# A two-phase recurrence and gated feed-forward kernel: the second phase's products in plain fp32 in place of three rounded products

## The chip, the cores and the metric

The kernel runs on one core of a Trainium2 chip. The metric is device time in microseconds (us) of one execution; lower is better. Engines are called as the profile calls them: PE is TensorE (matmul; PEld its weight loads), DVE VectorE, ACT ScalarE, POOL GpSimd, SP the engine that issues the DMAs (SPq in the profile).

## The reference

The first part is a recurrence over 768 steps for 4 batches x 8 heads with a 40 x 40 state; the second is a feed-forward block whose gate mixes along the sequence.

```python
for t in range(S):                                     # phase one
    y[:, :, t] = einsum('bhd,bhde->bhe', rt, state)
    Sa = einsum('bhde,bhe->bhd', state, at)
    state = state * wt[:, :, None, :] - Sa (x) bt + vt (x) kt
x = y as [batch 4, seq 768, 320]

h = maximum(x @ w_in, 0.0)                             # w_in 320 x 1024
u, v = h[..., :512], h[..., 512:]
v_n = (v - mean(v)) / sqrt(var(v) + 1e-06)
v_s = einsum('ts,bsd->btd', w_spatial, v_n) + b_spatial[None, :, None]   # phase two
return (u * v_s) @ w_out                               # w_out 512 x 320
```

All inputs and outputs are fp32; the two weight matrices w_in and w_out arrive as pairs of 32-bit words of float64 and are decoded on the chip.

## The kernel before

**Phase one** (`phase1`) computes the recurrence in 24 steps of 64 sequence positions, for two batches at a time, with many small fp32 matmuls (lines 536 to 638: 32 to 104 columns, 32 to 128 rows) and copies by ACT between them. Its order is a plan written out by hand: each operation has a due time, and the plan is sorted. Between the steps it also computes u and v (`m_u`, L753, and `m_v`, L708) for blocks of 128 positions, normalises v, and stores both to DRAM tensors `uts` and `vns`. For the second pair of batches this goes on after the last step, so that phase one has a tail. That tail and the second phase are ordered by the framework's scheduler, which places instructions by simulated time and interleaves the two.

**Phase two** (`phase2`) goes through 4 batches x 2 halves of the sequence (TH = 384 positions).

- Preparation: the six 128 x 768 tiles of the transposed w_spatial are loaded to a staging tile `raw` and split into a rounded high part `wsh` (ACT, `split_hi`, L50) and the remainder `wsl` (DVE, `split_lo`, L54). The four 128 x 320 blocks of w_out are decoded by `decode64` (seven DVE steps), and split into `woh` and `wol` in its last three operations (L96 to L98, one on ACT and two on POOL). Parts are of type fp32r, a rounded fp32 type that the matmul takes.
- `vload(b)` loads batch b's six 128 x 512 tiles of v to `raw`, splits each into `vh` (ACT) and `vl` (POOL), and loads u (`ut`). Tiles are kept for two batches; batch b+1 is loaded after the first half of batch b.
- `spatial(b, h)` makes four products pg (128 x 384), each a sum over six tiles of three matmuls: high x high (L173), high x low (L174), low x high (L175). DVE adds the bias (L177) and multiplies by u (L178) to give g; ACT and POOL split g into `gh` and `gl`.
- `proj(b, h)` makes three products po (128 x 320), each a sum over four blocks of three matmuls (L193). ACT copies them out (L194), and one DMA stores them. It is called one half late, so that the next half's spatial products stand ahead of it.

Counted over the whole phase this is 4 x 2 x 4 x 6 x 3 = 576 matmuls of 384 columns and 4 x 2 x 3 x 4 x 3 = 288 of 320 columns. Every DMA named is issued by SP, in one queue. The pools of phase two take memory that phase one's tiles used, and a tile waits for the tiles that were there.

Of the kernel before, what the change touches and what calls it, by code (L numbers as in the profile page):

```python
# [8 lines left out]
F32 = mybir.dt.float32  # L9
F32R = mybir.dt.float32r  # L10
# [4 lines left out]
ALU = mybir.AluOpType  # L15
# [3 lines left out]
P = 128  # L19
# [12 lines left out]
DH = 512  # L32

@with_exitstack
def tile_kernel(ctx, tc, early, late, vtok, win, wspT, bsp, wout, out):
    nc = tc.nc
    dram = ctx.enter_context(tc.tile_pool(name="dram", bufs=1, space=DRAM))
    B = out.shape[0]
    S = out.shape[1]
    xs = dram.tile([B, 2, NP, E, S], F32, name="xs")  # L40
    vns = dram.tile([B, S // P, P, DH], F32, name="vns")
    uts = dram.tile([B // NB, S // P, DH // P, P, NB, P], F32, name="uts")
    with ExitStack() as c1:
        phase1(c1, tc, early, late, vtok, win, xs, vns, uts, dram)
    with ExitStack() as c2:
        phase2(c2, tc, vns, uts, wspT, bsp, wout, out)


def split_hi(eng, hi, x):
    eng.activation(hi, x, AF.Copy)  # L50


def split_lo(eng, lo, x, hi):
    eng.tensor_tensor(out=lo, in0=x, in1=hi.bitcast(F32), op=ALU.subtract)  # L54


def decode64_steps(nc, pool, h, l, src, n, bufs=1):
    raw = pool.tile([P, n], I64, name="d_raw", bufs=2)
    nc.sync.dma_start(out=raw, in_=src)
    yield  # L60
    words = raw.bitcast(I32).rearrange("p (n two) -> p n two", two=2)
    lo, hi = words[:, :, 0], words[:, :, 1]
    t = [pool.tile([P, n], I32, name=f"d_t{i}", bufs=bufs) for i in range(3)]
    nc.vector.tensor_scalar(
        out=t[0], in0=hi, scalar1=3, scalar2=0x7FFFFFFF,
        op0=ALU.logical_shift_left, op1=ALU.bitwise_and,
    )
    yield
    nc.vector.tensor_scalar(
        out=t[1], in0=hi, scalar1=-0x80000000, scalar2=0x40000000,  # L70
        op0=ALU.bitwise_and, op1=ALU.bitwise_xor,
    )
    yield
    nc.vector.tensor_tensor(out=t[0], in0=t[0], in1=t[1], op=ALU.bitwise_xor)
    yield
    nc.vector.tensor_scalar(
        out=t[1], in0=hi, scalar1=0x7FFFFFFF, scalar2=None, op0=ALU.bitwise_and
    )
    yield
    f1 = t[2].bitcast(F32)  # L80
    nc.vector.scalar_tensor_tensor(
        out=f1, in0=t[1], scalar=float(897 << 20), in1=t[0].bitcast(F32),
        op0=ALU.is_ge, op1=ALU.mult,
    )
    yield
    nc.vector.tensor_scalar(
        out=t[0], in0=t[2], scalar1=-0x800000, scalar2=None, op0=ALU.bitwise_and
    )
    yield
    f2 = t[1].bitcast(F32)  # L90
    nc.vector.scalar_tensor_tensor(
        out=f2, in0=lo.bitcast(U32), scalar=2.0 ** -52, in1=t[0].bitcast(F32),
        op0=ALU.mult, op1=ALU.mult,
    )
    yield
    split_hi(nc.scalar, h, f1)  # L96
    nc.gpsimd.tensor_tensor(out=f1, in0=f1, in1=h.bitcast(F32), op=ALU.subtract)
    nc.gpsimd.tensor_tensor(out=l, in0=f1, in1=f2, op=ALU.add)  # L98


def decode64(*args, **kw):
    for _ in decode64_steps(*args, **kw):
        pass


def phase2(ctx, tc, vns, uts, wspT, bsp, wout, out):
    nc = tc.nc
    B, S, DO = out.shape
    NT = S // P
    TH = S // 2  # L110
    ND = DH // P

    def pool(name, bufs, **kw):
        return ctx.enter_context(tc.tile_pool(name=name, bufs=bufs, reuse_waits="tile", **kw))

    wstg = pool("p2r", 1)
    wsp = [pool(f"ws{i}", 1) for i in range(NT)]
    const = pool("p2c", 1)
    vp = [[pool(f"va{i}", 1, side="right") for i in range(NT)], None]
    up = [pool("ua", 1), None]  # L120
    stg = pool("p2s", 2)
    wp = pool("p2w", 2)
    vp[1] = [pool("vb", 1)] * NT
    up[1] = pool("ub", 1)
    ps_s = [pool(f"ps_s{i}", 2, space=PSUM) for i in range(2)]
    ps_o = pool("ps_o", 3, space=PSUM)

    wsh, wsl = [None] * NT, [None] * NT
    for i in range(NT):
        raw = wstg.tile([P, S], F32, name="raw", bufs=2)  # L130
        nc.sync.dma_start(out=raw, in_=wspT[i * P:(i + 1) * P])
        wsh[i] = wsp[i].tile([P, S], F32R, name=f"wsh{i}")
        wsl[i] = wsp[i].tile([P, S], F32R, name=f"wsl{i}")
        split_hi(nc.scalar, wsh[i], raw)
        split_lo(nc.vector, wsl[i], raw, wsh[i])
    woh = const.tile([P, ND, DO], F32R, name="woh")
    wol = const.tile([P, ND, DO], F32R, name="wol")
    for k in range(ND):
        decode64(nc, wstg, woh[:, k], wol[:, k], wout[k * P:(k + 1) * P], DO)
    bb = const.tile([P, S], F32, name="bb")  # L140
    nc.sync.dma_start(out=bb, in_=bsp.broadcast_to([P, S]))

    ut, vt = {}, {}

    def vload(b):
        vt[b] = []
        for i in range(NT):
            raw = wstg.tile([P, S], F32, name="raw", bufs=2)[:, 0:DH]
            nc.sync.dma_start(out=raw, in_=vns[b, i])
            vpool = vp[b % 2][i]  # L150
            h = vpool.tile([P, DH], F32R, name=f"vh{b % 2}{i}")
            l = vpool.tile([P, DH], F32R, name=f"vl{b % 2}{i}")
            split_hi(nc.scalar, h, raw)
            split_lo(nc.gpsimd, l, raw, h)
            vt[b].append((h, l))
        ut[b] = up[b % 2].tile([P, ND, S], F32, name=f"ut{b % 2}")
        for i in range(NT):
            nc.sync.dma_start(
                out=ut[b][:, :, i * P:(i + 1) * P],
                in_=uts[b // NB, i, :, :, b % NB].rearrange("d p t -> p d t"),  # L160
            )

    def spatial(b, h):
        ts = slice(h * TH, (h + 1) * TH)
        gh = wp.tile([P, ND, TH], F32R, name="gh")
        gl = wp.tile([P, ND, TH], F32R, name="gl")
        for d in range(ND):
            dc = slice(d * P, (d + 1) * P)
            pg = ps_s[d % 2].tile([P, TH], F32, name=f"pg{d % 2}")
            for i in range(NT):  # L170
                vh, vl = vt[b][i]
                w_h, w_l = wsh[i][:, ts], wsl[i][:, ts]
                nc.tensor.matmul(pg, lhsT=vh[:, dc], rhs=w_h, start=(i == 0), stop=False)  # L173
                nc.tensor.matmul(pg, lhsT=vh[:, dc], rhs=w_l, start=False, stop=False)  # L174
                nc.tensor.matmul(pg, lhsT=vl[:, dc], rhs=w_h, start=False, stop=(i == NT - 1))  # L175
            g = stg.tile([P, TH], F32, name="g")
            nc.vector.tensor_tensor(out=g, in0=pg, in1=bb[:, ts], op=ALU.add)  # L177
            nc.vector.tensor_tensor(out=g, in0=g, in1=ut[b][:, d, ts], op=ALU.mult)  # L178
            split_hi(nc.scalar, gh[:, d, :], g)
            split_lo(nc.gpsimd, gl[:, d, :], g, gh[:, d, :])  # L180
        return gh, gl

    def proj(b, h, gh, gl):
        ot = stg.tile([P, TH // P, DO], F32, name="ot")
        for j in range(TH // P):
            tc_ = slice(j * P, (j + 1) * P)
            po = ps_o.tile([P, DO], F32, name="po")
            mm = []
            for d in range(ND):
                mm += [(gh[:, d, tc_], woh[:, d, :]), (gh[:, d, tc_], wol[:, d, :]),  # L190
                       (gl[:, d, tc_], woh[:, d, :])]
            for i, (l, r) in enumerate(mm):
                nc.tensor.matmul(po, lhsT=l, rhs=r, start=(i == 0), stop=(i == len(mm) - 1))  # L193
            nc.scalar.activation(ot[:, j, :], po, AF.Copy)  # L194
        nc.sync.dma_start(
            out=out[b, h * TH:(h + 1) * TH].rearrange("(j p) n -> p j n", p=P), in_=ot
        )

    vload(0)
    pend = None  # L200
    for b in range(B):
        for h in range(2):
            gg = spatial(b, h)
            if b + 1 < B and h == 0:
                vload(b + 1)
            if pend is not None:
                proj(*pend)
            pend = (b, h, *gg)
    proj(*pend)


def phase1(ctx, tc, early, late, vtok, win, xs, vns, uts, dscr):
# [455 lines left out]
    def decode(half, k):  # L668
        cs = slice(half * DH, (half + 1) * DH)
        yield from decode64_steps(nc, st["dec"], wh[:, k, cs], wl[:, k, cs], win[:, k, cs], DH)  # L670
# [338 lines left out]
```

## Time and profile before

| what | value |
|---|---|
| median of 3 runs | 708.72 us (706.22 to 714.5) |
| profiled execution | span of 709.5 us from the first to the last instruction; the page lists no other time for it |
| instructions | 26133 |
| PE busy | 593.6 us (84%), 11136 matmuls |
| DVE busy | 437.5 us (62%) |
| ACT busy | 414.7 us (58%) |
| POOL busy | 290.3 us (41%) |
| mean granted TensorE clock | 0.900 |
| first and last matmul of phase two | start at 523.7 and 705.0 us |

A page of the profile lists busy time by engine, the span in 40 slices (a digit is the busy share in tenths), and groups of instructions by line of the kernel. In a group's row come line, engine, operation, output and inputs by tile names, shapes and count, then busy time in us and the mean duration of one in ns, then the idle time of the engine ahead of them and what ended it. The duration of a matmul reaches from its start to its modelled end and overlaps the next one's, so what one costs in a dense stream is the distance of starts. A row of the timeline has start, length, engine, line, operation and count; a row of the chain of work that ended last has start, its share of the chain's time, engine, tile, line and count.

### The profile page before, as it was taken

What the parts mean: (1) busy time and instruction counts of PE and PEld (TensorE: products, weight loads), DVE (VectorE), ACT (ScalarE), POOL (GpSimd) and SP (SyncE); (2) the same over time, 40 slices, a digit from 0 to 9 for tenths busy, and PEclk for the clock granted to TensorE, in tenths of its full rate; (3) what the DMA queues carried; (4) which work ended last, traced back from release to release, by engine and by line L of the source; (5) the groups of instructions that cost most, each with busy time, mean ns of one, the idle gap of its engine ahead of it and who ended that gap; (6) DMA issues with size and microseconds to landing.
All of it is one profiled execution on the core that took longest, in us unless ns stands there. A gap on an engine that the chain in (4) does not pass through costs nothing. (4 is left out here: it accounts for less than half of the span.)

```text
span 709.5 us, 26133 instructions
## 1 busy us (share of the span) xinstructions
PE 593.6 (84%) x11136; PEld 538.4 (76%) x11136; DVE 437.5 (62%) x862; ACT 414.7 (58%) x904; POOL 290.3 (41%) x486
## 2 busy tenths in 40 slices
PE   1707886587877789898997999999999999999997
PEld 1606785476766678787886788778888988999997
DVE  7897659977999899766688456612127521332221
ACT  2406754375565777587886889889855543331112
POOL 4102213212345444253464524545457982453221
PEclk9656978787797877899999899999999999999999
DMA  8443665273554724456536434344336454650001
GB/s 188 84 97 56 122 144 103 63 154 73 121 113 93 141 66 115 96 125 127 122 109 209 119 118 121 94 125 138 99 103 186 144 170 129 203 176 29 29 29 55
DMA packets 101339, 81.38 MB, mean 115 GB/s; under 512 B 33576, under 2 KB 90152, under 8 KB 99304
## 3 DMA queue, kind: packets, MB, share of 16 engines
q1 hardware_dynamic: 100680, 78.01, 44.0%
q10 hardware_dynamic: 544, 1.72, 1.1%
q8 instruction: 87, 1.43, 0.9%
q14 instruction: 28, 0.23, 0.1%
HBM read 59.20 MB, written 20.50 MB: 112 GB/s over the span
## 5 line engine op out<-in xcount | busy, mean ns | idle before, releaser
L397 POOL TENSOR_SCALAR_AFFINE_SELECT Rt<-Rt 64x512 f32<-64x512 f32 (+1 forms) x144 | 84.0, 585 | 99.4 <-ACT Rt L583 76.3
L546 ACT ACTIVATE Rt<-bp 64x416 f32<-64x416 f32 x96 | 49.1, 512 | 71.5 <-PE bp L536 69.5
L352 DVE TENSOR_TENSOR itmp<-A 128x30 f32<-128x30 f32 (+9 forms) x180 | 75.3, 419 | 3.2
L397 POOL TENSOR_SCALAR_AFFINE_SELECT At<-At 64x512 f32<-64x512 f32 x48 | 36.3, 756 | 96.5 <-ACT At L407 94.3
L536 PE MATMUL bp<-lin,Mc 40*64 40x104 f32 x768 | 53.5, 302 | 15.4 <-DVE y L651 11.7
L173 PE MATMUL pg<-wsh,vh 128*128 128x384 f32 x192 | 64.7, 337 | 0.0
L174 PE MATMUL pg<-wsl,vh 128*128 128x384 f32 x192 | 64.7, 337 | 0.0
L175 PE MATMUL pg<-wsh,vl 128*128 128x384 f32 x192 | 64.6, 336 | 0.0
L356 DVE TENSOR_TENSOR A<-A,itmp 128x30 f32<-128x30 f32 (+9 forms) x180 | 59.0, 328 | 6.2
L536 PEld LDWEIGHTS bp<-lin,Mc 40*64 40x64 f32 x768 | 46.7, 168 | 18.3 <-DVE y L651 13.7
L177 DVE TENSOR_TENSOR g<-pg,bb 128x384 f32<-128x384 f32 x32 | 17.8, 556 | 62.9 <-PE pg L175 59.1
L54 POOL TENSOR_TENSOR gl<-g,gh 128x384 fp32r<-128x384 f32 x32 | 33.9, 1064 | 50.2 <-ACT gh L50 50.0
L583 ACT ACTIVATE Rt<-ch 64x416 f32<-64x416 f32 x96 | 49.2, 512 | 4.5 <-PE ch L572 2.1
L554 PE MATMUL ch<-Rt,At 128*64 128x104 f32 x768 | 47.5, 283 | 0.0
L554 PEld LDWEIGHTS ch<-Rt,At 128*64 128x64 f32 x768 | 42.1, 158 | 4.5 <-issue 1.9
L50 ACT ACTIVATE gh<-g 128x384 fp32r<-128x384 f32 x32 | 16.6, 522 | 48.9 <-DVE g L178 48.8
L442 PE MATMUL bk<-ident,sl 128*128 128x128 f32 x192 | 31.1, 293 | 16.3 <-ACT tk L448 6.8
L572 PE MATMUL ch<-ffs,xf 64*64 64x104 f32 x768 | 43.4, 267 | 0.1
L54 POOL TENSOR_TENSOR vl<-raw,vh 128x512 fp32r<-128x512 f32 x24 | 32.3, 1353 | 26.2 <-ACT vh L50 13.9
L716 DVE BATCH_NORM_STATS2 bs<-vr 128x6 f32<-128x512 f32 x24 | 16.6, 691 | 41.6 <-ACT vr L710 41.5
L638 PE MATMUL bp<-Rt,tk 128*40 128x64 f32 x768 | 32.5, 240 | 10.1 <-issue 10.1
L572 PEld LDWEIGHTS ch<-ffs,xf 64*64 64x64 f32 x768 | 38.3, 143 | 1.4 <-ACT Rt L583 0.2
(138 smaller groups left out, 1575.5 us busy)
## 6 DMA issues: line engine op xcount, KB each, us to landing
ein<-in_early SPq DMA_DIRECT2D x40, 387.0 KB
lin<-in_late SPq DMA_DIRECT2D x48, 160.0 KB
uts<-ur SPq DMA_DIRECT2D x48, 128.0 KB
vns<-vr SPq DMA_DIRECT2D x24, 256.0 KB
raw<-vns SPq DMA_DIRECT2D x24, 256.0 KB
ut<-uts SPq DMA_DIRECT2D x24, 256.0 KB
Rt<-in_vtok SPq DMA_DIRECT2D x48, 80.0 KB
xs<-y SPq DMA_DIRECT2D x48, 80.0 KB
```

The costliest lines, as they stand in the source:

```text
L54: eng.tensor_tensor(out=lo, in0=x, in1=hi.bitcast(F32), op=ALU.subtract)
L173: nc.tensor.matmul(pg, lhsT=vh[:, dc], rhs=w_h, start=(i == 0), stop=False)
L174: nc.tensor.matmul(pg, lhsT=vh[:, dc], rhs=w_l, start=False, stop=False)
L175: nc.tensor.matmul(pg, lhsT=vl[:, dc], rhs=w_h, start=False, stop=(i == NT - 1))
L352: nc.vector.tensor_tensor(out=tp, in0=A[:, k + 1:, k:k + 1].broadcast_to([P, m, k]), in1=A[:, k:k + 1, 0:k].broadcast_to([P, m, k]), op=AL ...
L356: nc.vector.tensor_tensor(out=A[:, k + 1:, 0:k], in0=A[:, k + 1:, 0:k], in1=tp, op=ALU.add)
L397: nc.gpsimd.affine_select(out=t, in_=t, pattern=[[0, k], [1, C]], base=0, channel_multiplier=-1, compare_op=ALU.is_gt, fill=0.0,)
L536: nc.tensor.matmul(bp[PR[par], q, :], lhsT=Mc[RR[par], n, :], rhs=li[RR[par], n, C:], start=(q == 0), stop=False, skip_group_check=True,)
L546: nc.scalar.activation(Rt[par][PR[par], gp, :], st["bp", g][PR[par]], AF.Copy)
L554: nc.tensor.matmul(ff[PR[1 - par], q, :], lhsT=At[par][:, n, :], rhs=Rt[par][:, n, :], start=True, stop=True,)
L572: nc.tensor.matmul(xx[ev, q, :], lhsT=xf[ev, n, :], rhs=ffs[ev, q, :], start=True, stop=True,)
L583: nc.scalar.activation(Rt[par][PR[par], gp], xx[PR[1 - par]], AF.Copy, scale=-1.0)
```

## The change

Each sum of three rounded products becomes one product of the fp32 tiles themselves. The tiles `ws`, `v`, `gt` and `wo` take the place of the pairs of high and low parts; the splits are left out. w_spatial and v are loaded by DMA straight into the tiles that the matmul reads. `decode64` is called with no low part and then ends in one POOL addition. A helper `product` issues the matmuls; with COLS = 128 its inner loop runs once, over the full width.

```diff
@@ decode64_steps
     yield
+    if l is None:
+        nc.gpsimd.tensor_tensor(out=h, in0=f1, in1=f2, op=ALU.add)
+        return
     split_hi(nc.scalar, h, f1)
@@ phase2
-    wsh, wsl = [None] * NT, [None] * NT
+    ws = []
     for i in range(NT):
-        raw = wstg.tile([P, S], F32, name="raw", bufs=2)
-        nc.sync.dma_start(out=raw, in_=wspT[i * P:(i + 1) * P])
-        wsh[i] = wsp[i].tile([P, S], F32R, name=f"wsh{i}")
-        wsl[i] = wsp[i].tile([P, S], F32R, name=f"wsl{i}")
-        split_hi(nc.scalar, wsh[i], raw)
-        split_lo(nc.vector, wsl[i], raw, wsh[i])
-    woh = const.tile([P, ND, DO], F32R, name="woh")
-    wol = const.tile([P, ND, DO], F32R, name="wol")
+        w = wsp[i].tile([P, S], F32, name=f"ws{i}")
+        nc.sync.dma_start(out=w, in_=wspT[i * P:(i + 1) * P])
+        ws.append(w)
+    wo = const.tile([P, ND, DO], F32, name="wo")
     for k in range(ND):
-        decode64(nc, wstg, woh[:, k], wol[:, k], wout[k * P:(k + 1) * P], DO)
+        decode64(nc, wstg, wo[:, k], None, wout[k * P:(k + 1) * P], DO)
...
     def vload(b):
         for i in range(NT):
-            raw = wstg.tile([P, S], F32, name="raw", bufs=2)[:, 0:DH]
-            nc.sync.dma_start(out=raw, in_=vns[b, i])
-            vpool = vp[b % 2][i]
-            h = vpool.tile([P, DH], F32R, name=f"vh{b % 2}{i}")
-            l = vpool.tile([P, DH], F32R, name=f"vl{b % 2}{i}")
-            split_hi(nc.scalar, h, raw)
-            split_lo(nc.gpsimd, l, raw, h)
-            vt[b].append((h, l))
+            t = vp[b % 2][i].tile([P, DH], F32, name=f"v{b % 2}{i}")
+            nc.sync.dma_start(out=t, in_=vns[b, i])
+            vt[b].append(t)
...
+    def product(o, terms):
+        for j, (l, r) in enumerate(terms):
+            for c in range(0, P, COLS):
+                cs = slice(c, c + COLS)
+                nc.tensor.matmul(
+                    o[cs], lhsT=l[:, cs], rhs=r, start=(j == 0), stop=(j == len(terms) - 1)
+                )
+
     def spatial(b, h):
-        gh = wp.tile([P, ND, TH], F32R, name="gh")
-        gl = wp.tile([P, ND, TH], F32R, name="gl")
+        gt = wp.tile([P, ND, TH], F32, name="gt")
         for d in range(ND):
-            for i in range(NT):
-                vh, vl = vt[b][i]
-                w_h, w_l = wsh[i][:, ts], wsl[i][:, ts]
-                nc.tensor.matmul(pg, lhsT=vh[:, dc], rhs=w_h, start=(i == 0), stop=False)
-                nc.tensor.matmul(pg, lhsT=vh[:, dc], rhs=w_l, start=False, stop=False)
-                nc.tensor.matmul(pg, lhsT=vl[:, dc], rhs=w_h, start=False, stop=(i == NT - 1))
+            product(pg, [(vt[b][i][:, dc], ws[i][:, ts]) for i in range(NT)])
             g = stg.tile([P, TH], F32, name="g")
             nc.vector.tensor_tensor(out=g, in0=pg, in1=bb[:, ts], op=ALU.add)
-            nc.vector.tensor_tensor(out=g, in0=g, in1=ut[b][:, d, ts], op=ALU.mult)
-            split_hi(nc.scalar, gh[:, d, :], g)
-            split_lo(nc.gpsimd, gl[:, d, :], g, gh[:, d, :])
+            nc.vector.tensor_tensor(out=gt[:, d, :], in0=g, in1=ut[b][:, d, ts], op=ALU.mult)
...
     def proj(b, h, gt):
-            for d in range(ND):
-                mm += [(gh[:, d, tc_], woh[:, d, :]), (gh[:, d, tc_], wol[:, d, :]),
-                       (gl[:, d, tc_], woh[:, d, :])]
-            for i, (l, r) in enumerate(mm):
-                nc.tensor.matmul(po, lhsT=l, rhs=r, start=(i == 0), stop=(i == len(mm) - 1))
+            product(po, [(gt[:, d, tc_], wo[:, d, :]) for d in range(ND)])
```

More of the change, by code (lines that the diff above doesn't have):

```diff
@@ L111, in phase2 @@
     ND = DH // P
+    COLS = 128
     def pool(name, bufs, **kw):
@@ L169, in spatial, with proj @@
             pg = ps_s[d % 2].tile([P, TH], F32, name=f"pg{d % 2}")
-            for i in range(NT):
-                vh, vl = vt[b][i]
-                w_h, w_l = wsh[i][:, ts], wsl[i][:, ts]
-                nc.tensor.matmul(pg, lhsT=vh[:, dc], rhs=w_h, start=(i == 0), stop=False)
-                nc.tensor.matmul(pg, lhsT=vh[:, dc], rhs=w_l, start=False, stop=False)
-                nc.tensor.matmul(pg, lhsT=vl[:, dc], rhs=w_h, start=False, stop=(i == NT - 1))
+            product(pg, [(vt[b][i][:, dc], ws[i][:, ts]) for i in range(NT)])
             g = stg.tile([P, TH], F32, name="g")
             nc.vector.tensor_tensor(out=g, in0=pg, in1=bb[:, ts], op=ALU.add)
-            nc.vector.tensor_tensor(out=g, in0=g, in1=ut[b][:, d, ts], op=ALU.mult)
-            split_hi(nc.scalar, gh[:, d, :], g)
-            split_lo(nc.gpsimd, gl[:, d, :], g, gh[:, d, :])
-        return gh, gl
-    def proj(b, h, gh, gl):
+            nc.vector.tensor_tensor(out=gt[:, d, :], in0=g, in1=ut[b][:, d, ts], op=ALU.mult)
+        return (gt,)
+    def proj(b, h, gt):
         ot = stg.tile([P, TH // P, DO], F32, name="ot")
@@ L187, in proj @@
             po = ps_o.tile([P, DO], F32, name="po")
-            mm = []
-            for d in range(ND):
-                mm += [(gh[:, d, tc_], woh[:, d, :]), (gh[:, d, tc_], wol[:, d, :]),
-                       (gl[:, d, tc_], woh[:, d, :])]
-            for i, (l, r) in enumerate(mm):
-                nc.tensor.matmul(po, lhsT=l, rhs=r, start=(i == 0), stop=(i == len(mm) - 1))
+            product(po, [(gt[:, d, tc_], wo[:, d, :]) for d in range(ND)])
             nc.scalar.activation(ot[:, j, :], po, AF.Copy)
```

## The prediction

> **What bounds the kernel now.** I read the page's table of slices first, then the busy times by stretch, then the groups of the last stretch, then single instructions in order of time. The slices show a TensorE (PE) that is full from about slice 28 to the end, at a granted clock of 9 tenths or more. The stretch of interest begins when the first product of the second phase (L173) starts, at 523.67 us. The columns of the stretches are length, then busy time and count of PE, PEld, DVE, ACT, POOL, then granted clock and DMA.
>
> ```profile
> span 709.5 us, 26133 instructions
> ...
> PE   1707886587877789898997999999999999999997
> ...
> 523.67:582.00 58.33, 58.33 (x421) 53.54 (x420) 27.84 (x55) 29.54 (x61) 44.61 (x71) 1.00 0.52 154
> 582.00:608.00 26.00, 24.20 (x147) 22.48 (x145) 4.62 (x13) 8.57 (x20) 9.17 (x30) 1.00 0.61 184
> 608.00:705.30 97.30, 97.20 (x598) 96.69 (x596) 26.82 (x46) 25.04 (x53) 32.67 (x30) 1.00 0.23 75
> ```
>
> In these 181.6 us PE idles 1.9 us (1.8 in the middle row, 0.1 in the last) and DVE, ACT and POOL are at most 76% busy (POOL's 44.61 of 58.33). A busy PE need not be at its peak, so the next view asks what it does: the matmul groups of that stretch, and two timeline rows for each of the two shapes.
>
> ```profile
> L173 PE MATMUL pg<-wsh,vh 128*128 128x384 f32 x192 | 64.7, 337 | 0.0
> L174 PE MATMUL pg<-wsl,vh 128*128 128x384 f32 x192 | 64.7, 337 | 0.0
> L175 PE MATMUL pg<-wsh,vl 128*128 128x384 f32 x192 | 64.6, 336 | 0.0
> L193 PE MATMUL po<-woh,gh 128*128 128x320 f32 x96 | 29.8, 310 | 0.1
> L193 PE MATMUL po<-woh,gl 128*128 128x320 f32 x96 | 29.7, 309 | 0.0
> L193 PE MATMUL po<-wol,gh 128*128 128x320 f32 x96 | 29.6, 309 | 0.0
> ...
> 648.11 0.34 PE L173 MATMUL pg<-wsh,vh 128*128 128x384 f32 x1
> ...
> 650.71 0.34 PE L173 MATMUL pg<-wsh,vh 128*128 128x384 f32 x1
> ...
> 624.82 0.31 PE L193 MATMUL po<-woh,gh 128*128 128x320 f32 x1
> ...
> 628.78 0.34 PE L173 MATMUL pg<-wsh,vh 128*128 128x384 f32 x1
> ```
>
> The durations overlap: 15 matmuls lie from 648.11 to 650.71, so one 384-column matmul starts every 0.1733 us though each is listed with 0.337. In the same way 27 matmuls of 320 columns fill 624.82 to 628.78, 0.1467 us each. The sum that PE must walk through is 576 x 0.1733 = 99.8 and 288 x 0.1467 = 42.2, together **142.1 us** of the 181.6. The other 37.6 us are what is left of phase one (L753, L708 and the scan's chunk products), woven between. PE is the bound, by its starts, and what follows it is short:
>
> ```profile
> 694.77 10.57 PE po L193 x72
> 705.36 0.44 ACT ot L194
> ...
> 705.83 0.37 SPq L195 DMA_DIRECT2D out_y<-ot  x1
> ```
>
> From the last matmul's end to the end of the span are 4.1 us of copy and store, which the change leaves alone.
>
> **The change part by part.**
>
> *The products.* Per pair of tiles three matmuls of rounded type become one of plain fp32: 192 of 384 columns and 96 of 320. The trace of before has no full-width fp32 product of two data tiles, but phase one has many narrower ones (L554, L572) and fp32 transposes at full width (L442).
>
> ```profile
> L572 PE MATMUL ch<-ffs,xf x768: 246/249/430, 62.6 to 535.7; 64*64 64x104 f32 x192
> L442 PE MATMUL bk<-ident,sl x192: 272/273/476, 20.7 to 509.7; 128*128 128x128 f32 x192
> ...
> 511.95 0.52 PE L572 MATMUL ch<-ffs,xf 64*64 64x104 f32 x8
> 509.22 0.49 PE L442 MATMUL bk<-ident,sl 128*128 128x128 f32 x3
> ...
> 507.33 1.58 PE ch L554 x32
> ...
> 528.21 0.86 PE ch L554 x16
> ```
>
> Count first. The code issues L572's matmul 24 steps x 2 groups x 4 heads x 2 halves = 384 times; the row has x768. An fp32 product is therefore **two records**; a transpose (24 x 8 = 192, row x192) is one. Then the time of a record. Three transposes take 0.49 us from first start to last end, and the last lasts 0.273, so the pitch is (0.49 - 0.273)/2 = 0.1085 us for 128 columns. L554 with 16 more records (8 more products of 104 columns) takes 1.58 - 0.86 = 0.72 us more, 0.090 us for one product. L554 and L572 send alternate products to different halves of the array. Eight records of L572 last 0.52 us; if they start in side-by-side pairs there are three steps of (0.52 - 0.249)/3 = 0.090 us, and this is one record's time, two of which make a product. If they start evenly, seven steps of 0.039 us, a product takes half of that. The listed durations speak for pairs: rounded matmuls go from 309 ns at 320 columns to 337 at 384, 0.44 ns a column, so their fixed part is about 169 ns, and a 104-column fp32 record has 249 - 169 = 80 ns, 0.77 ns a column, the transpose 104 ns, 0.81. The transposes' pitch at full width says the same without any pairing: 0.85 ns a column.
>
> So the unknown, a full-width fp32 record, lies between 0.43 ns a column (even starts) and, for an upper end, twice the rounded matmul's slope, 0.875 ns. I take 0.833 ns a column plus 2.5 ns, the line that gives both pitches (104 columns: 89 ns; 128: 109 ns), since the L442 row is the nearest in shape. A 384-column record is then 0.3225 us, a product 0.645, against three rounded ones at 0.520; a 320-column product 0.538 against 0.440. New sum: 192 x 0.645 = 123.8 and 96 x 0.538 = 51.7, together 175.5 us. **Plus 33.4 us**, all on PE, in a stretch in which PE is full.
>
> *Weight loads.* Each record has its own load, 576 where there were 864. The next load starts with the matmul that runs, and lies under it:
>
> ```profile
> 704.58 0.31 PE L193 MATMUL po<-woh,gl 128*128 128x320 f32 x1
> 704.58 0.19 PEld L193 LDWEIGHTS po<-woh,gh 128*128 128x128 f32 x1
> ```
>
> A 0.32 us record covers 0.19 more easily than a 0.15 us one. Cost nothing; uncovered, see the rivals.
>
> *The splits of v and g.* ACT and POOL lose these, with their kin for the weights:
>
> ```profile
> L54 POOL TENSOR_TENSOR gl<-g,gh 128x384 fp32r<-128x384 f32 x32 | 33.9, 1064 | 50.2 <-ACT gh L50 50.0
> L50 ACT ACTIVATE gh<-g 128x384 fp32r<-128x384 f32 x32 | 16.6, 522 | 48.9 <-DVE g L178 48.8
> L54 POOL TENSOR_TENSOR vl<-raw,vh 128x512 fp32r<-128x512 f32 x24 | 32.3, 1353 | 26.2 <-ACT vh L50 13.9
> ```
>
> All this lies beside a full PE, so by itself it is worth nothing after 523 us, except for the 1.9 us in which PE idles, most of it behind ACT:
>
> ```profile
> PE pv L753 <- ACT ur L755: 1.0, 1, 1.0
> ...
> PE itmp L753 <- ACT vr L710: 0.8, 1, 0.8
> ```
>
> With fewer splits ACT comes to these copies sooner, and batches 0 and 1 alone give PE 16.7 us more to do meanwhile (half of 33.4). I take 1 us of the 1.9 as gained.
>
> *Splits inside phase one.* Before 523 us ACT makes the wsh tiles and six of the vh, among the copies that the scan waits for:
>
> ```profile
> 457.40 0.83 ACT L50 ACTIVATE wsh<-raw 128x768 fp32r<-128x768 f32 x1
> ...
> 514.25 1.15 ACT L50 ACTIVATE vh<-raw 128x512 fp32r<-128x512 f32 x2
> ...
> PE ch L612 <- ACT Rt L583: 3.7, 6, 1.1
> PE bk L505 <- ACT zt L487: 1.1, 4, 0.3
> PE bk L442 <- ACT xf L514: 1.0, 1, 1.0
> PE bk L442 <- ACT At L407: 0.8, 3, 0.4
> ```
>
> Between 400 and 523 us PE waits 6.6 us in all for ACT (the last four rows), which is the most that lighter ACT could return, since a split delays only what happens to queue behind it. Four wsh and six vh at these durations are 4 x 0.83 + 3 x 1.15 = 6.8 us, few of them just ahead of a copy that PE waits for, so I take 1.5 us, and keep 0 and 6.6 as ends.
>
> *Moved loads.* v now lands in its tile directly, so the DMA of batch 2 or 3 waits until PE has read batch 0 or 1, where before it could land in a staging buffer and the split waited. The DMA sits on SP's queue, ahead of the ut loads, output stores and phase one's last stores and loads. Batch b+2 is needed only after another batch's two halves, over 30 us of PE work, so I cost it at nothing; if that cover were gone, six loads of 2.7 us to landing, mostly overlapping, would show as a PE gap of 3 to 10 us. SBUF shrinks (one tile in place of two), so tiles come free no later.
>
> *wout's decoding* loses an ACT copy and one of two POOL steps per block; off the path, nothing.
>
> Sum: 33.4 - 1.0 - 1.5 = **+30.9 us**. The profiled execution's span becomes 740.4. The page gives no time for it beyond its span; the three timed runs have 706.22 to 714.5 with a median of 708.72, 0.8 under the span, so the forecast of the median is 708.72 + 30.9 = **739.6 us**.
>
> **The rivals.**
>
> *A product needs only half of what I take (faster).* The place is the same 288 products; the point is whether L572's records run side by side or one after another. If evenly, a product is 0.3225 and 0.269 us, the sum 87.8, 54.3 us less than now: 708.72 - 54.3 = **654.4**. The last batch's data would not forbid it: it lands at 603.6, and half of 87.8 and 4.1 after that are 651.6.
>
> ```profile
> 600.89 2.67 DMA raw<-vns
> ```
>
> Against it are the transposes' 0.1085 us and the durations, for it only that no full-width pair was seen. The Trainium skill, "Perfetto Trace Analysis", section "Engine Utilization", says that the array's output rate is divided by 2 for FP32_LOW_HIGH; taken as the rate of a whole fp32 product that gives this rival's time. By that rule each record agrees, at 0.85 ns a column against 0.44, but the trace shows two such records for each product (x768), so I hold the division to be per record. Chance 5%, and 1% more for a change that does not do what it says (one rounded record per product: bounded by 603.6 + 23.7 + 4.1, about 631).
>
> *The fp32 weight load does not hide at full width (slower still).* For it: fp32 products in the trace load 64 columns at most. Against: L442 loads 128 and keeps its pitch. Its load row has a median of 140 ns; all 576 exposed would be 80.6 us, **820**. Chance 5%.
>
> ```profile
> L442 PEld LDWEIGHTS bk<-ident,sl x192: 137/140/231, 20.6 to 509.5; 128*128 128x128 f32 x192
> ```
>
> *The granted clock falls under dense fp32.* In the third hundred microseconds, with fp32 work alone, it was 0.81:
>
> ```profile
> 200.00:300.00 100.00, 81.55 (x2090) 73.77 (x2088) 91.87 (x167) 64.70 (x143) 41.50 (x50) 0.81 0.48 101
> ```
>
> Those stretches have a PE with gaps; where it is full the clock is 1.00. At 0.81 the 213 us of PE work (175.5 + 37.6) grow by 50: **790**. Chance 4%.
>
> *A new wait.* The direct loads stall PE, or the order of phase one's tail between longer products leaves a gap over 13 us: beyond 753, chance 4%. *No change* would need a product of about 0.52 us, for which no row speaks: 2%.
>
> **How the numbers follow.** The forecast has 79%, at 739.6. Its own ends: low, 33.4 - 1.9 - 6.6 = +24.9, 733.6, and 4 us more for a phase one that the order of instructions happens to favour, so 729; high, records at 0.875 ns a column (192 x 0.677 + 96 x 0.565 = 184.2 with the 2.5 ns kept, +42.1) and no gain, 750.8, with 2 us for gaps, 753. The cases outside make up about 20%, so 729 to 753 is the range. 1% (7 us) is about what a measurement of this kernel can tell from no change. Faster 0.06 (first rival and its 1%), same 0.02, slower 0.92.
>
> **What would show it.** In the changed kernel's profile: 384 records of 384 columns and 192 of 320 columns in the second phase; starts 0.32 and 0.27 us apart; no second-phase fp32r tile on ACT or POOL; PE without a gap over 1 us after the first product, which starts at 520 to 524 us; the last matmul at about 735 us. The forecast is wrong if the starts are closer to 0.16 us (first rival), if PEld stands idle-free and PE not (second), if the clock is under 0.95 after 530 us, or if gaps sum to over 10 us.

## The result, and the profile after

The changed kernel takes **743.9 us** (median of four runs, 739.4 to 745.4) against 708.4 (706.2 to 714.5) for the kernel before: a ratio of 1.048, 95% interval 1.043 to 1.054. The forecast was 739.6, with a range of 729 to 753.

The page's head and slices, the stretches from the first product on (length, then busy time and count of PE, PEld, DVE, ACT, POOL, then clock and DMA), the two matmul groups, and the last two pieces of PE in the chain that ended last, all of the changed kernel:

```profile
span 743.1 us, 25349 instructions
PE 619.0 (83%) x10848; PEld 500.3 (67%) x10848; DVE 425.0 (57%) x856; ACT 379.9 (51%) x838; POOL 221.7 (30%) x426
...
PE   2507884669677777989989969999999999999997
```

```profile
526.20:582.00 55.80, 55.76 (x325) 37.62 (x324) 13.26 (x28) 15.57 (x32) 12.44 (x36) 1.00 0.49 150
582.00:608.00 26.00, 26.00 (x107) 17.81 (x106) 4.15 (x11) 5.57 (x13) 5.55 (x20) 1.00 0.28 86
608.00:738.10 130.10, 130.09 (x460) 84.89 (x459) 27.02 (x52) 15.38 (x34) 3.36 (x17) 1.00 0.20 66
```

```profile
L162 PE MATMUL pg<-ws,v 128*128 128x384 f32 x384 | 127.3, 487 | 0.0
L162 PE MATMUL po<-wo,gt 128*128 128x320 f32 x192 | 52.7, 433 | 0.0
```

```profile
709.69 15.48 PE pg L162 x48
725.17 12.94 PE po L162 x48
```

The counts are the forecast ones, 384 and 192 records for 192 and 96 products. These two pieces of the chain give the price: 15.48/48 = **0.3225 us** for a record of 384 columns and 12.94/48 = **0.2696 us** for one of 320, where 0.3225 and 0.269 were forecast. PE no longer idles at all (0.05 us in 211.9), the clock is 1.00, and POOL, 44.6 us busy in the first stretch before, has 12.4. The first product starts at 526.2 us, later than the 520 to 524 that the prediction named as a sign. The weight loads, listed with 0.19 us each, leave no gap on PE.

The span grew by 33.6 us. Where they arose is read from a mark that both profiles have, the first of the 32 records of `c_xx` in a step of phase one (steps counted from 0; L572 before, L562 after). The rows are those of steps 17, 18 and 22, first of the kernel before:

```profile
418.91 1.64 PE L572 MATMUL ch<-ffs,xf 64*64 64x104 f32 x32
...
437.65 1.55 PE L572 MATMUL ch<-ffs,xf 64*64 64x104 f32 x30
...
511.64 1.55 PE L572 MATMUL ch<-ffs,xf 64*64 64x104 f32 x30
```

and of the changed kernel:

```profile
419.07 1.64 PE L562 MATMUL ch<-ffs,xf 64*64 64x104 f32 x32
...
444.52 1.64 PE L562 MATMUL ch<-ffs,xf 64*64 64x104 f32 x32
...
514.96 1.64 PE L562 MATMUL ch<-ffs,xf 64*64 64x104 f32 x32
```

| piece, us | before | after | difference |
|---|---|---|---|
| start to step 17 | 418.9 | 419.1 | +0.2 |
| step 17 to 18 | 18.7 | 25.4 | **+6.7** |
| step 18 to 22 | 74.0 | 70.4 | **-3.6** |
| step 22 to the first product | 12.0 | 11.2 | -0.8 |
| first product to the last one's start | 181.3 | 211.5 | **+30.1** |
| from there to the end | 4.5 | 5.4 | +1.0 |

The second phase grew by what its products cost, less the gaps, close to the forecast; but phase one, which holds none of these products, gained and lost several microseconds. The loss is one wait. Of the changed kernel, who waited for whom on PE between 418 and 446 us, and DVE in order of time around it:

```profile
PE bp L526 <- DVE y L641: 6.1, 1, 6.1
```

```profile
429.51 0.47 DVE L91 SCALAR_TENSOR_TENSOR d_t<-d_raw,d_t 128x320 f32<-128x320 uint32 x1
...
430.29 0.97 DVE L64 TENSOR_SCALAR d_t<-d_raw 128x320 int32<-128x320 int32 x1
431.18 0.39 DVE L346 TENSOR_TENSOR A<-A,itmp 128x240 f32<-128x240 f32 x1
431.50 1.40 DVE L69 TENSOR_SCALAR d_t<-d_raw 128x320 int32<-128x320 int32 x1
432.93 0.93 DVE L74 TENSOR_TENSOR d_t<-d_t,d_t 128x320 int32<-128x320 int32 x1
433.79 0.41 DVE L641 TENSOR_TENSOR y<-bp,Et 104x256 f32<-104x256 f32 x1
```

The d_t rows (L64 to L91) are the decoding of w_out. PE cannot start the next step's bp before DVE has taken y out of its bank, and y stands in DVE's queue behind four steps of the decoding that cost 3.8 us here (L64 and L69 take some three times as long as at 424 us of the same execution, 0.33 and 0.51; why was not followed up). In the kernel before, the decoding ended in phase one's tail, where PE waited for none of it. The rows are those of the decoding's POOL step at L97, one for each block of w_out, with first and last start, of the kernel before and of the changed kernel:

```profile
L97 POOL TENSOR_TENSOR d_t<-d_t,woh x4: 867/1056/1147, 533.0 to 555.0; 128x320 f32<-128x320 f32 x4
```

```profile
L97 POOL TENSOR_TENSOR wo<-d_t,d_t x4: 857/942/1031, 419.3 to 436.9; 128x320 f32<-128x320 f32 x4
```

The explanation offered is that the scheduler placed the decoding earlier because the smaller tiles of the changed kernel lie where phase one's memory comes free early. Experiment 1 puts it to the test.

### The profile page after: what moved, and what is told of

Same layout as the page of the kernel before. It is cut to its first block, busy times and chain, and to the rows that moved or that the text cites. A ratio compares the mean times of both kernels' runs of the same rounds, so it can differ in the third digit from the quotient of the medians.

```text
span 743.1 us, 25349 instructions
## 1 busy us (share of the span) xinstructions
PE 619.0 (83%) x10848; PEld 500.3 (67%) x10848; DVE 425.0 (57%) x856; ACT 379.9 (51%) x838; POOL 221.7 (30%) x426
## 5 line engine op out<-in xcount | busy, mean ns | idle before, releaser
L162 PE MATMUL pg<-ws,v 128*128 128x384 f32 x384 | 127.3, 487 | 0.0
L162 PEld LDWEIGHTS pg<-ws,v 128*128 128x128 f32 x384 | 72.3, 190 | 47.2
L526 PE MATMUL bp<-lin,Mc 40*64 40x104 f32 x768 | 51.4, 294 | 19.0 <-DVE y L641 15.4
L184 ACT ACTIVATE ot<-po 128x320 f32<-128x320 f32 x24 | 10.5, 436 | 107.0 <-PE po L162 107.0
L526 PEld LDWEIGHTS bp<-lin,Mc 40*64 40x64 f32 x768 | 44.6, 162 | 22.3 <-DVE y L641 17.4
L162 PE MATMUL po<-wo,gt 128*128 128x320 f32 x192 | 52.7, 433 | 0.0
L162 PEld LDWEIGHTS po<-wo,gt 128*128 128x128 f32 x192 | 36.6, 190 | 15.6
L432 PE MATMUL bk<-ident,sl 128*128 128x128 f32 x192 | 31.6, 297 | 16.9 <-ACT tk L438 6.9
L544 PE MATMUL ch<-Rt,At 128*64 128x104 f32 x768 | 45.3, 272 | 0.2
L562 PE MATMUL ch<-ffs,xf 64*64 64x104 f32 x768 | 44.5, 272 | 0.6 <-issue 0.6
L544 PEld LDWEIGHTS ch<-Rt,At 128*64 128x64 f32 x768 | 39.7, 150 | 5.7 <-issue 1.6
L317 PE MATMUL bk<-at,sl 64*32 64x32 f32 x1536 | 23.1, 214 | 23.7 <-DVE sl L304 14.1
L562 PEld LDWEIGHTS ch<-ffs,xf 64*64 64x64 f32 x768 | 39.5, 147 | 2.2 <-issue 1.1
```

What stands on the lines that cost most here:

```text
L162: nc.tensor.matmul(o[cs], lhsT=l[:, cs], rhs=r, start=(j == 0), stop=(j == len(terms) - 1))
L317: nc.tensor.matmul(pl[o:o + HB, n, :], lhsT=sl[PR[par], n, par, cs], rhs=at[PR[par], n, cs], start=True, stop=True,)
L432: nc.tensor.transpose(pt[:, n, :], sl[:, h * NP + n].rearrange("p q c -> p (q c)"), ident)
L526: nc.tensor.matmul(bp[PR[par], q, :], lhsT=Mc[RR[par], n, :], rhs=li[RR[par], n, C:], start=(q == 0), stop=False, skip_group_check=True,)
L544: nc.tensor.matmul(ff[PR[1 - par], q, :], lhsT=At[par][:, n, :], rhs=Rt[par][:, n, :], start=True, stop=True,)
L562: nc.tensor.matmul(xx[ev, q, :], lhsT=xf[ev, n, :], rhs=ffs[ev, q, :], start=True, stop=True,)
```

## The experiments

**1. The changed kernel again, and the old layout.** The first is the control. The second doubles the new tiles and uses half of each, which puts the pools where they were; no instruction is added or taken away:

```diff
-        w = wsp[i].tile([P, S], F32, name=f"ws{i}")
+        w = wsp[i].tile([P, 2 * S], F32, name=f"ws{i}")[:, 0:S]
...
-    wo = const.tile([P, ND, DO], F32, name="wo")
+    wo = const.tile([P, 2 * ND, DO], F32, name="wo")[:, 0:ND]
...
-            t = vp[b % 2][i].tile([P, DH], F32, name=f"v{b % 2}{i}")
+            t = vp[b % 2][i].tile([P, 2 * DH], F32, name=f"v{b % 2}{i}")[:, 0:DH]
...
-        gt = wp.tile([P, ND, TH], F32, name="gt")
+        gt = wp.tile([P, 2 * ND, TH], F32, name="gt")[:, 0:ND]
```

> The changed kernel itself, beside the others on the same chip. Product theory: +33 us of PE work in the second phase and a 6 us stall of PE in phase one; 740 to 746 us, and the stall at the step near 430 us is there again, since the order of instructions on each engine is fixed. Rival (the stall was an accident of one execution): phase one reaches its step 18 as early as before, and the time is near 738.

> The changed kernel with its tiles ws, wo, v and gt made twice as large (half of each unused), so that the second phase's pools lie where they lay before; the instructions are the same, and the decoding of w_out stands behind phase one's last steps on DVE. Memory theory: the smaller tiles let the decoding move into phase one, where DVE's y of one step waits behind it and PE idles 6.1 us; with the old layout that wait is gone and the time falls by 4 to 6 us, to 738 to 740. Rival (the 2.5 us later first product comes from something else): 743 to 745 as before this edit, first product still at 526.

The control took 742.3 us (ratio 1.043, interval 1.035 to 1.052), as expected. The old layout took **731.2** (1.036, 1.030 to 1.042), below the 738 to 740 expected. The kernel before took 707.3 on that chip. The marks of steps 17, 18 and 22, first of the control, then of the old layout:

```profile
411.86 1.64 PE L562 MATMUL ch<-ffs,xf 64*64 64x104 f32 x32
437.79 1.64 PE L562 MATMUL ch<-ffs,xf 64*64 64x104 f32 x32
508.25 1.64 PE L562 MATMUL ch<-ffs,xf 64*64 64x104 f32 x32
```

```profile
411.69 1.64 PE L562 MATMUL ch<-ffs,xf 64*64 64x104 f32 x32
430.24 1.47 PE L562 MATMUL ch<-ffs,xf 64*64 64x104 f32 x28
500.71 1.47 PE L562 MATMUL ch<-ffs,xf 64*64 64x104 f32 x28
```

Step 17 to 18 takes 25.9 us again in the control and 18.6 with the old layout, while 18 to 22 stays at 70.5 in both. PE's wait for y between 411 and 431 us of the old layout is down to a tenth,

```profile
PE bp L526 <- DVE y L641: 0.6, 1, 0.6
```

and the decoding stands behind step 22 again:

```profile
L97 POOL TENSOR_TENSOR wo<-d_t,d_t x4: 855/857/993, 510.0 to 522.8; 128x320 f32<-128x320 f32 x4
```

So the wait belongs to the placement of the decoding, and the placement to the tiles' size; step 17 to 18 is 7.4 us shorter without it. It is the marks that show this. The ratios differ by 0.7% (5 us), their intervals overlap, and executions scatter ahead of step 17 (the changed kernel's two profiled executions reached step 11 at 300.6 and 296.0 us, the old layout's at 290.9).

**2. One stage alone.** Spatial products as before, the projection in fp32; the splits of g and of w_out go with it:

```diff
-                mm += [(gh[:, d, tc_], woh[:, d, :]), (gh[:, d, tc_], wol[:, d, :]),
-                       (gl[:, d, tc_], woh[:, d, :])]
+                mm += [(gt[:, d, tc_], wo[:, d, :])]
```

> Only the output projection in plain fp32 (96 products of 320 columns), the spatial product in three rounded ones. Price by record: 96 x (0.538 - 0.440) = +9.4 us, minus at most 1 us for the splits of g that go: 716 to 718 against 708. Rival (the price is not per product but a property of the spatial stage, such as the direct loads of v): no more than +2, 708 to 711.

714.1 us, ratio 1.010 (1.006 to 1.014): +6.8 where +8.4 to +9.4 was expected, outside the 716 to 718. From first product to last start it is 186.9 us, +5.5. The records cost what they should, and PE's idle time of before is gone here too:

```profile
691.98 12.93 PE po L191 x48
```

```profile
517.59:704.90 187.31, 187.31 (x1066) 167.01 (x1064) 54.96 (x109) 46.38 (x96) 46.74 (x95) 1.00 0.35 110
```

The price is per product. Of the 9.4 us, 1.9 are the idle time that went (1 us was taken); the other 2 are not resolved. Some 0.9 of them may be work that now stands before the first product (step 22 to it takes 12.9 us, 12.0 before).

**3. The splits added again as dead work,** twice: those of v and g into tiles of a pool of their own, and, for v alone and with the old layout, into tiles that come free early. The lines shown are those for v; the remark in them is not in the code.

```diff
             nc.sync.dma_start(out=t, in_=vns[b, i])
+            dh = wstg.tile([P, DH], F32R, name="dvh", bufs=2)     # first version: pool "dead"
+            dl = wstg.tile([P, DH], F32R, name="dvl", bufs=2)
+            split_hi(nc.scalar, dh, t)
+            split_lo(nc.gpsimd, dl, t, dh)
```

> The changed kernel with the splits of v and g added again by ACT and POOL, into tiles that nobody reads. Theory (the splits of v cost phase one time on ACT): from step 18 to step 22 phase one takes about 74 us as before, where the changed kernel takes 70.4; the second phase stays at 211 us from first to last product, so the time rises by 3 to 4 us. Rival (the 3.6 us come from the moved loads or the layout): 70.4 stays, and so does the time.

> The version with the old layout, and the splits of v added again by ACT and POOL into two small tiles that nobody reads; these lie in memory that comes free early, so that batch 0's six splits stand in phase one's ACT queue, between the copies that the scan waits for. Theory (the 3.5 us that phase one gains from step 18 to 22 are the splits of v on ACT): 73.5 to 74 us there as before, where the old layout has 70.5, PE waits again for the copy of the scan ahead of the state update (3 to 4 us in all), and the second phase keeps its 210.5 us. Rival (the gain comes from the moved loads or from w_spatial's splits): 70.5 stays.

The first took 737.6 us (ratio 1.044, 1.038 to 1.050) and its steps 18 to 22 stayed at 70.5, as the rival had it. But it did not test what it was made for: all its splits of v were placed after 534 us. What it shows instead is the price of splits beside a full PE. In the second phase ACT and POOL have 66.0 and 83.6 us to do, where the control has 36.5 and 21.4, and the stretch from first to last product is the same:

```profile
520.35:731.80 211.45, 211.41 (x889) 140.22 (x887) 46.85 (x91) 66.03 (x134) 83.61 (x129) 1.00 0.29 91
```

The second (736.2 us against 706.6 for the kernel before, ratio 1.047, 1.038 to 1.055) has its splits in phase one. Its marks of steps 18 and 22, and PE's wait between them:

```profile
428.31 1.64 PE L566 MATMUL ch<-ffs,xf 64*64 64x104 f32 x32
505.38 1.64 PE L566 MATMUL ch<-ffs,xf 64*64 64x104 f32 x32
```

```profile
PE ch L606 <- ACT Rt L577: 3.5, 2, 2.7
```

77.1 us in place of 70.5: the direction and PE's wait (3.5 us for the copy ahead of the state update) are as expected, the size is 3 us over it. Of the 6.6 us more, 5.5 lie in step 20 (23.4 us against 18.0), in which ACT stands 2.0 us in front of two splits for their own loads (in brackets):

```profile
469.18 0.63 ACT L50 ACTIVATE dvh<-v 128x512 fp32r<-128x512 f32 x1 [0.84 <-DMA v<-vns]
471.01 0.63 ACT L50 ACTIVATE dvh<-v 128x512 fp32r<-128x512 f32 x1 [1.20 <-DMA v<-vns]
```

The rest of that step's excess was not followed up. The kernel before has these splits between the marks (wsh are w_spatial's):

```profile
439.58 0.84 ACT L50 ACTIVATE wsh<-raw 128x768 fp32r<-128x768 f32 x1
456.87 0.63 ACT L50 ACTIVATE vh<-raw 128x512 fp32r<-128x512 f32 x1
...
477.59 1.14 ACT L50 ACTIVATE vh<-raw 128x512 fp32r<-128x512 f32 x2
496.04 0.63 ACT L50 ACTIVATE vh<-raw 128x512 fp32r<-128x512 f32 x1
```

With the wsh at 457.40 that is one split in step 18, two in 19, two in 20, one in 21; the changed kernel's four steps are 0.65, 1.22, 1.01 and 0.67 us shorter. A split thus costs phase one 0.5 to 0.7 us. The splits of w_spatial have a half on DVE as well (wsl), and the last version of experiment 5 tells the two apart: it rounds w_spatial on ACT, has no wsl and splits no v. Its step 18, with one such split on ACT at 432.09 us, takes 17.75 us, as before; its steps 20 and 21, with none, take 18.0 and 16.9, as in the changed kernel. So ACT's part is what counts. Its step 19 takes 20.4 us, 1.9 more than in the changed kernel with one split; there ACT also stands 1.2 us idle ahead of it.

**4. The halves of the array.** COLS = 64 makes each product as two, on the two halves.

```diff
-    COLS = 128
+    COLS = 64
```

> The changed kernel with COLS = 64: each product is made as two products of half the output columns, 1152 records where there were 576. Pair theory (two halves of the array run side by side, each record 0.833 ns a column): records start in pairs, a pair 0.32 us after the last, the sum stays near 175 us and the time at 738 to 746. Rival (the halves run one after another, and phase one's pairs of starts show nothing): the sum doubles, some 915.

747.3 us (ratio 1.058, 1.051 to 1.064), 1.3 above the upper end expected. Of the chain that ended last:

```profile
712.47 15.48 PE pg L162 x96
727.95 12.93 PE po L162 x96
```

Twice the records in the same 15.48 and 12.93 us: the halves run side by side, so phase one's pairs of starts did show a record's full time, and the first rival, whose point this was and which the pitch of 0.3225 us already spoke against, falls. The 9 us that the stretch is longer (220.5) lie in its first part, where the products are mixed with phase one's tail; that was not followed up.

**5. What a pass costs by type, and what lies under PE.** Three versions. The first is the kernel before with parts in bf16 in place of fp32r, which makes the parts less exact. The second is the kernel before with one rounded product, the other two left out. The third makes the same one product without low parts at all; it is built from the changed kernel, with its tiles in fp32r at their old places, v rounded where phase one writes it and loaded straight into its tile, and g rounded by DVE's multiply. The lines shown come from all three; the remark in them is not in the code.

```diff
-        wsh[i] = wsp[i].tile([P, S], F32R, name=f"wsh{i}")
+        wsh[i] = wsp[i].tile([P, 2 * S], BF16, name=f"wsh{i}")[:, 0:S]
...
-                nc.tensor.matmul(pg, lhsT=vh[:, dc], rhs=w_h, start=(i == 0), stop=False)
-                nc.tensor.matmul(pg, lhsT=vh[:, dc], rhs=w_l, start=False, stop=False)
-                nc.tensor.matmul(pg, lhsT=vl[:, dc], rhs=w_h, start=False, stop=(i == NT - 1))
+                nc.tensor.matmul(pg, lhsT=vh[:, dc], rhs=w_h, start=(i == 0), stop=(i == NT - 1))
...
-        nc.scalar.activation(vr, vr, AF.Identity, bias=q[:, 2:3], scale=q[:, 1:2])
+        nc.scalar.activation(vo, vr, AF.Identity, bias=q[:, 2:3], scale=q[:, 1:2])   # vo is F32R
```

> The kernel of before with its parts in bf16 in place of fp32r, still three products (high and low part have 8 bits each, so the product is less exact), tiles padded to their old size. Count theory (what matters is passes times columns, and the pass of a 2-byte type has no extra cost of its own): a 384-column matmul starts every 0.1625 us where fp32r takes 0.1733, a 320-column one every 0.136 where it takes 0.1467; 9 us less, 698 to 700 against 707. Rival (fp32r's extra is the weight load or the array, and stays): 707.

> The kernel of before with one rounded product per pair (high x high) in place of three; both other products are left out, the splits stay. PE sum 142.1 / 3 = 47.4 us, 94.7 less. If PE alone were the bound: 614. Chain theory: the last results of phase one set the floor (last v lands at 603.6 before, then half of 47.4 and 4.1 us of copy and store), 625 to 640, and PE shows gaps of some 20 us between 540 and 610.

> One rounded (fp32r) product per pair, the low parts not made at all: v is rounded where phase one normalises it, g by DVE's multiply, w_out by its last addition, w_spatial by ACT; tiles at their old places. Two of three products are left out, so it is less exact. Chain theory: the second phase is bound by the tail of phase one, which now passes fewer POOL and ACT operations: below the 653 of the version that keeps the splits, 638 to 650. Rival (the tail is bound by its DMAs and PE's own order, not by splits): 650 to 655.

bf16: **698.1 us** against 707.7, ratio 0.988 (0.983 to 0.993), as expected. Two timeline rows, 24 matmuls apart, 0.1625 us each as expected, and the stretch from the first product on:

```profile
639.81 0.33 PE L178 MATMUL pg<-wsh,vh 128*128 128x384 bf16 x1
...
643.71 0.33 PE L178 MATMUL pg<-wsh,vh 128*128 128x384 bf16 x1
```

```profile
513.26:689.30 176.04, 171.06 (x1162) 115.85 (x1160) 59.22 (x113) 62.55 (x133) 79.17 (x131) 0.99 0.39 120
```

The price of a matmul came out; that the total hit as well is in part luck. In the profile PE idles 5.0 us in this stretch, 1.9 before, so the second phase is only some 5.6 us shorter, where the sum of matmuls fell by 9.3. The interval of the ratio (5 to 12 us) holds both.

One rounded product: 653.6 us against 707.3, ratio 0.926 (0.919 to 0.934), outside the expected 625 to 640. The floor expected rested on a row misread: the load that lands at 603.6 us in the kernel before is the last of batch 2. Batch 3's last load is issued there at 630.91, and in this version ACT splits that tile at 625.82:

```profile
630.91 0.33 SPq L149 DMA_DIRECT2D raw<-vns  x1
```

```profile
625.82 0.62 ACT L50 ACTIVATE vh<-raw 128x512 fp32r<-128x512 f32 x1
```

PE's sum fell by 94.7 us and the time by 53.7. With the cover gone, PE waits 27.5 us from 517 to 647 us, most of it for ACT and DVE, which stand in the chain of splits; between 540 and 610 us, where PE is 74% busy, the granted clock is 0.88 as well:

```profile
PE pv L750 <- ACT vr L707: 8.6, 4, 4.2
PE po L190 <- ACT gh L50: 7.7, 12, 2.1
PE pg L173 <- DVE g L175: 6.0, 8, 3.3
```

```profile
540.00:610.00 70.00, 51.82 (x249) 43.35 (x248) 30.88 (x51) 31.06 (x69) 46.94 (x82) 0.88 0.53 170
```

Without the low parts the same products take **613.4 us**, ratio 0.869 (0.864 to 0.873), below the 638 expected. Its stretches from the first product on:

```profile
515.40:540.00 24.60, 23.91 (x217) 20.29 (x216) 15.92 (x40) 11.76 (x25) 11.64 (x30) 1.00 0.62 190
540.00:575.00 35.00, 32.46 (x195) 29.35 (x194) 12.28 (x30) 16.24 (x36) 13.28 (x47) 1.00 0.85 260
575.00:604.00 29.00, 28.86 (x176) 28.59 (x175) 21.19 (x43) 6.83 (x18) 0.00 (x0) 1.00 0.75 252
```

PE is 96% busy there, 85.2 of 88.6 us, and the clock is 1.00. Phase one's tail ends sooner too: the last v is stored at 575 us and loaded at 581, where the kernel before had 608 and 631. Its waits for splits are gone, but the direct loads of v and the clock changed with them, and what each is worth was not separated. Both bf16 and single-product versions give up exactness that three products or fp32 keep.

## Why the prediction was right or wrong

- *Products, +33.4 us: right.* 384 x 0.3225 + 192 x 0.2696 = 175.6 us, where 175.5 was forecast. Two records a product, each 0.833 ns a column plus 2.5 ns, hold at full width. That the price came out to the digit is more than the rows of before could give: a line through the two pitches exactly (0.090 us at 104 columns, 0.1085 at 128) has 0.771 ns a column plus 9.8 ns, and would have made it +24.6 us. The lower end of 0.43 ns (even starts) fell with the pitch, and experiment 4 shows why. The Trainium skill, "FP8 and Floating Point Precision", section "TensorE Precision Notes", gives true fp32 as four passes through the array; the runs agree, 0.645 us for a product of 384 columns against 0.1625 for one bf16 matmul (experiment 5). The division by 2 in the Trainium skill, "Perfetto Trace Analysis", section "Engine Utilization", fits a record (0.3225 us against 0.1625) and not a product.
- *Gaps, -1.0: too small.* The stretch from first product to last start grew by 30.1, not 32.4. PE's 1.9 us of idle time went entirely; the remaining 1.4 us were not resolved.
- *Splits beside a full PE cost nothing: right,* shown by the dead work of experiment 3 (211.5 us with it and 211.9 without).
- *Splits inside phase one, -1.5: too small.* The part that can be compared, step 18 to the first product, gained 4.4 us, within the bound of 6.6. The splits of steps 18 to 21 cost 0.5 to 0.7 us each, where the prediction took few of them to stand ahead of a copy that PE waits for.
- *wout's decoding, "off the path, nothing": the step that failed.* It was costed where it stood, in the tail. The change moved it, by its memory alone, into phase one, in front of y on DVE: +6.7 us. "SBUF shrinks, so tiles come free no later" was true, and its consequence, that work then comes earlier into queues that are already full, was not drawn.
- *Moved loads and weight loads at nothing: right.* The changed kernel's PE has no gap in the second phase; the records keep their pitch over loads of 0.19 us. The clock stayed at 1.00.
- *A row misread in the first rival.* The load that lands at 603.6 us is not the last batch's (experiment 5); batch 3's v is still being stored at 608.1 and its loads are issued up to 630.9. Only the rivals used it, not the forecast.
- *The sum.* +30.9 forecast, +33.6 in the profile: -2.3 for the gaps, +1.0 from the last product's start on, +6.7 for y, -2.9 for phase one's lighter ACT beyond the 1.5, and 0.2 before step 17. The medians differ by 35.5, inside the interval of 30 to 38 that the ratio gives.

The sign of the forecast rested on the price of a record alone; that the total came within 5 us rested also on two errors of phase one, +6.7 and -2.9, that partly cancelled.

## What to carry to other kernels

Price a change of number format in records times columns, read from the distance of starts of the nearest shape: here one fp32 product of 384 columns costs 1.24 times three fp32r ones, whatever the count of instructions says. When tiles shrink, look at what the scheduler can now do earlier and in whose queue it will stand; padding a tile back to its old size is a cheap test, and here it was worth 7 us of phase one. Before paying for more exactness, and where the result may be less exact, a single rounded product without the low parts was the largest gain here; with it went the splits in the chain that fed PE, behind which the version that keeps them waited some 22 us.

## What the runs showed of the hardware that was not expected

A matmul of the rounded fp32 type starts 0.011 us later after the last one than a bf16 matmul does, at both widths: 0.1733 us for 384 columns where bf16 takes 0.1625, and 0.1467 for 320 where bf16 takes 0.136 (72 of them in 9.79 us). One fp32 record takes 0.3225 us for 384 columns, 1.98 times the bf16 matmul. The weight loads were listed with about 0.19 us for fp32r and fp32 alike and with 0.098 in bf16; whether the 0.011 us belong to the load or to the array was not separated. Products on half the array, two records side by side at a time, keep exactly the full-width time in a dense stretch (15.48 us for 24 products of 384 columns in both).
